# Keys of heads 0 to 3 of the second batch through the DMA crossbar, and a new order of crossings, joins, sends and loads around them

## The chip, the core and the metric

The kernel runs on one core of a Trainium2 chip. The metric is device time in microseconds (us) of one execution. "Span" is the profiled part of one execution, some 1.8 us shorter than its time; positions in a trace are counted from its start.

## The reference

Clustered attention (4 batches, 8 heads, 768 rows of 64), whose output goes straight into a mixture of 4 experts. A key counts for a query only where both have the same nearest centroid of 16.

```python
q_assign = argmax(einsum('bhsd,hcd->bhsc', q_n, c_n))      # keys likewise
mask = q_assign[:, :, :, None] == k_assign[:, :, None, :]
attn = softmax(where(mask, q @ k.T / sqrt(D), -1e9))
x = (attn @ v) as [3072, 512]
out = sum over e of p[:, e] * (relu(x @ w1[e]) @ w2[e])     # 4 experts, w1 512x1024, w2 1024x512
```

## The kernel before

Three jobs are interleaved. TensorE does the attention of a batch, the expert products of the batch before, and the preparation ("assignment") of the next batch: queries and keys must be turned so that head dimension lies along partitions, scored against the centroids, and their one-hot cluster numbers written below them as 16 more rows, so that one product gives both score and mask.

There are two ways to turn a float32 block. TensorE can do it against an identity (`turn`). Or it goes round TensorE: GpSimd splits the 32-bit values into two 16-bit halves (`split`), the DMA crossbar transposes the halves, issued by the SP queue (`cross`), and GpSimd joins them (`merge`):

```python
class Crossed(Assign):
    def split(self, n):
        if n == 0:
            self.h16 = self.halves(raws.tile([128, HG, QW], F32, name="h16", tag="raw"))
        ...                                            # cut: pool() copies, L361 or L364
    def cross(self, j):
        if j == 0:
            self.t16 = self.halves(raws.tile([128, HG, QW], F32, name="t16", tag="raw"))
        ...
        nc.sync.dma_start(out=self.t16[:, c]..., in_=self.h16[:, c]..., transpose=True)    # L371
    def merge(self, n):
        ...                                            # cut: pool() copies into self.all, L380
```

`h16` and `t16` come from the same ring of five buffers (`raws`) that queries, keys and values are loaded into. After the joins come the product with the centroids (`scores`, L267), its turn back (`back`, L276), the maximum and one-hot on VectorE (`top`), the crossing of the one-hot (`cross_onehot`, L426) and sixteen small DMAs that put it in place, issued by GpSimd (`send_all`, L336). GpSimd also issues the 1 MB loads of the expert weights (`load_w`, L153 and L154).

Preparation of a batch is a list of numbered items, taken one after the other between pieces of TensorE's main work. `put(n, f)` hangs `f` on item n; within an engine the order of items is the order of issue. For the second batch (b == 1), with y = 0 to 3 for keys of heads 0 to 3, queries of heads 0 to 3, keys of heads 4 to 7, queries of heads 4 to 7:

```python
g, z = divmod(y, 2)
if g == 0:
    for j in range(HG):
        put(4 * z + j, lambda x=x, j=j: turn(x, j))
else:
    for j in range(HG):
        put((8, 14)[z] + j, lambda x=x, j=j: x.split(j))
        put((13, 18)[z] + j, lambda x=x, j=j: x.cross(j))
        put((20, 24)[z] + j, lambda x=x, j=j: x.merge(j))
    ...
```

The softmax here doesn't subtract the row's maximum and nothing guards it: scores larger than these inputs give would overflow.

Of the kernel before, what the change touches and what calls it, by code (L numbers as in the profile page):

```python
# [20 lines left out]
def kernel(  # L21
# [27 lines left out]
    HG = H // 2  # L49
# [79 lines left out]
    def load_part(b, t, g, js=slice(0, HG), c=slice(0, A * D)):  # L129
        nc.sync.dma_start(  # L130
            out=raw[b, t, g][:, js, c],
            in_=(q, k, v)[t][b, g * HG:(g + 1) * HG]
            .rearrange("h (p a) d -> p h (a d)", p=128)[:, js, c])

    def take_raw():
        nonlocal loaded
        x = ORDER[loaded]
        loaded += 1
        raw[x] = raws.tile([128, HG, A * D], F32, name="raw")
        return x  # L140

    def load_raw(n=1, upto=len(ORDER)):
        for _ in range(n):
            if loaded < upto:
                load_part(*take_raw())

    def cast_v(b, g, js=range(HG)):
        for j in js:
            pool(VX[b % 2][:, g * HG + j, :, :D],
                 raw[b, 2, g][:, j, :].rearrange("p (a d) -> p a d", d=D))  # L150

    def load_w(e):
        nc.gpsimd.dma_start(out=W1[e], in_=moe_w1[e].rearrange("(i p) f -> p i f", p=128))  # L153
        nc.gpsimd.dma_start(out=W2[e], in_=moe_w2[e].rearrange("(i p) f -> p i f", p=128))  # L154
# [57 lines left out]
    class Assign:  # L212
# [23 lines left out]
        def turn(self, y, copy, shared=False):  # L236
            tp = self.bank()
            m, w = self.m, self.w
            for x in range(m):
                for i in range(self.i0, self.i1):  # L240
                    c0 = x * w + (i - self.i0) * 128
                    nc.tensor.matmul(tp[:, c0:c0 + 128],  # L242
                                     raw[self.b, self.t, self.g][:, y * m + x,
                                                                 i * 128:(i + 1) * 128],
                                     ident, is_transpose=True)
            if shared:
                t32 = moe.tile([128, DM], F32, name="t32q", tag="oacc", bufs=4)
            else:
                if self.all is None:
                    self.all = asg.tile([128, HG * QW], F32, name="t32", bufs=2)  # L250
                t32 = self.all[:, y * w:(y + 1) * w]
            copy(t32, tp[:, :m * w])
            self.t32s.append(t32)
# [63 lines left out]
        def put(self, j, r, on):  # L317

            p0 = 2 * CL * j
            self.move(self.rows(slice(D, D + CL), j, r),  # L320
                      self.ot[p0:p0 + CL, r * self.w:(r + 1) * self.w], on)
# [22 lines left out]
    class Crossed(Assign):  # L344
# [41 lines left out]
        def casts(self):  # L386
            y = self.g * HG // 2
            if self.b < ROWS:
                for r in range(2):
                    self.cast_half(r)  # L390
                return
            dve(late(self.t, self.b)[:, y:y + HG // 2], self.rows_of())
# [71 lines left out]
    def assigns(b):  # L464


        xs = [Crossed(b, t, g, (("misc",), ("mo",))[t == 0])
              for t, g in ((1, 0), (0, 0), (1, 1), (0, 1))]
        todo = {}

        def put(at, *fs):
            todo.setdefault(at, []).extend(fs)

        def turn(x, j):
            x.turn(j, dve)
            for r in range(2):
                x.cast(j, r, pool)

        if b == 1:
            for y, x in enumerate(xs):  # L480
                g, z = divmod(y, 2)
                if g == 0:
                    for j in range(HG):
                        put(4 * z + j, lambda x=x, j=j: turn(x, j))
                else:
                    for j in range(HG):
                        put((8, 14)[z] + j, lambda x=x, j=j: x.split(j))
                        put((13, 18)[z] + j, lambda x=x, j=j: x.cross(j))
                        put((20, 24)[z] + j, lambda x=x, j=j: x.merge(j))
                    put((24, 28)[z], x.take_all)  # L490
                    for r in range(2):
                        put(28 + 3 * z + r, lambda x=x, r=r: x.cast_half(r))
                at = (8, 29)[g]
                put(at, lambda x=x: x.scores(dve))
                put(at + 1 + z, x.back, x.top, x.scale_onehot, x.cross_onehot)
                put(at + (4, 5)[g] + z, x.send_all)
            put(1, lambda: load_w(2))
            put(3, lambda: load_raw(upto=11))
            put(20, lambda: cast_v(b, 0))
            put(22, lambda: load_raw(2, upto=13))  # L500
            put(24, lambda: load_w(3))
            put(30, lambda: cast_v(b, 1))

        for y, x in enumerate(xs if b > 1 else ()):
            z = y % 2
            t = 8 * y
            for j in range(HG):
                put(t + j, lambda x=x, j=j: x.split(j))
                put(t + 2 + j, lambda x=x, j=j: x.cross(j))
                put(t + 9 + j, lambda x=x, j=j: x.merge(j))  # L510
            put(t + 6, load_raw)
            put(t + 15 + 4 * z, x.casts)
            at = 16 * (y // 2) + 24
            put(at, lambda x=x, t=("mo", "misc")[z]: x.scores_split(t))
            put(at + 2 + 6 * z, x.cross_scores)
            put(at + 5 + 6 * z, x.merge_scores)
            if b < ROWS:
                put(at + 9 + 6 * z, x.top, x.scale_onehot, x.cross_onehot)
                put(at + 13 + 6 * z, x.send_all)
                continue  # L520
            put(at + 9 + 6 * z, x.top, x.number, x.cross_numbers)
            put(at + 12 + 6 * z, x.store_numbers)
            put(at + 14 + 6 * z, x.spread_numbers)
        for g in range(2 if b > 1 else 0):
            for j in range(HG):
                put(36 + 8 * g + j, lambda g=g, j=j: cast_v(b, g, (j,)))
            put(40 + 8 * g, load_raw)
        for at in range(XSTEPS[b]):
            for f in todo.pop(at, []):
                f()  # L530
            yield
        assert not todo
# [248 lines left out]
    NSTEP = B * UB * PER_U + PAUSE  # L781
    PER_B = UB * PER_U
    LEAD = 6
    XSTEPS = [0, 38, 63, 63]
    step = 0
    gens = []

# [101 lines left out]
    def late_queries():  # L889
        load_raw()  # L890
        for y in (0, 1):
            qd.turn(y, dve, True)
            yield
        casts(qd, (0, 1))
        load_raw(3)
        qd.scores(dve)
        yield
        qd.back()
        qd.top()
        yield  # L900
        qd.onehot()
        qd.keep()
        qd.send_all()
        yield
    S1 = PER_U + PAUSE
    gens.append(Paced(late_queries(), 5, S1 - 6, S1 + 4))
    for b in range(1, B):
        gens.append(Paced(assigns(b), XSTEPS[b], PER_B * (b - 1) if b > 1 else S1 + 7,
                          PER_B * b - 2 if b > 1 else S1 + 55))
# [54 lines left out]
```

## Time and profile before

| | before |
|---|---|
| time, median of 3 | 472.60 us |
| TensorE busy | 463.2 of 470.4 us |
| TensorE's share of the chain that ended last | 95% |
| GpSimd busy | 194.8 us |
| VectorE busy | 227.4 us |

The number to read is the first of TensorE: the kernel is a row of matmuls with hardly a gap. Two rows of the page, in 40 equal slices of the span (11.8 us each; a digit is tenths), show the same for the whole length: busy share, then granted clock.

```profile
PE   8999999999999999999999999999999999999996
PEclk9999999999999999999999999999999999999999
```

The list of TensorE's waits (engine, tile, line, releaser: total us, times, longest) has only small entries. This, its largest, is from the first microseconds.

```profile
PE ps_s L87 <- DVE blank L80: 1.2, 1, 1.2
```

Two stretches of the SP queue (start, duration, line, operation): the second batch's second keys are loaded, and their crossings come right behind the one-hot crossings.

```profile
33.97 0.46 SPq L130 DMA_DIRECT2D raw<-in_k_dram  x1
...
57.03 2.79 SPq L426 DMA_TRANSPOSE oht<-oh  x2
59.93 2.57 SPq L371 DMA_TRANSPOSE t<-h  x2
```

### The profile page before, as it was taken

How to read it: one execution, taken by the hardware profiler on the slowest of the kernel's cores; microseconds unless marked ns; L12 is line 12 of the kernel's file. 1: busy time of each engine (PE TensorE's matmuls, PEld its weight loads, DVE VectorE, ACT ScalarE, POOL GpSimd, SP SyncE). 2: the span in 40 equal slices, each digit the busy share in tenths (PEclk: the TensorE clock that was granted, in tenths of full speed). 3: DMA queues.
4: the chain of work that ended last, by engine and by line, in shares of the span. 5: the costliest groups of instructions: out<-in, count | busy, mean ns of one | idle time of the engine just before them, and what ended most of it. 6: DMA issues, size and time to landing. Idle time of an engine off the chain costs nothing.

```text
span 470.4 us, 11349 instructions
## 1 busy us (share of the span) xinstructions
PE 463.2 (98%) x4505; PEld 329.1 (70%) x4505; DVE 227.4 (48%) x554; ACT 276.9 (59%) x502; POOL 194.8 (41%) x301
## 2 busy tenths in 40 slices
PE   8999999999999999999999999999999999999996
PEld 5778777767767766777776667766766666667665
DVE  5964723542325563321234463523778767674112
ACT  5767675445655655566565656656665675664342
POOL 5936779275355593450433942000233232230000
PEclk9999999999999999999999999999999999999999
DMA  8999966996645941503666844220100100100101
GB/s 277 262 211 339 216 99 120 236 127 182 144 68 127 182 114 32 144 18 61 169 123 127 133 106 151 71 75 11 52 13 8 54 11 10 33 29 11 46 2 45
DMA packets 82381, 49.85 MB, mean 106 GB/s; under 512 B 57944, under 2 KB 77080, under 8 KB 82328
## 3 DMA queue, kind: packets, MB, share of 16 engines
q1 hardware_dynamic: 73080, 39.80, 35.1%
q0 software_dynamic: 8576, 9.25, 11.0%
q8 instruction: 35, 0.57, 0.5%
q14 instruction: 18, 0.15, 0.1%
q10 hardware_dynamic: 672, 0.08, 0.1%
HBM read 37.31 MB, written 6.30 MB: 93 GB/s over the span
## 4 chain that ended last, share of the span: by engine, by line
PE 95%; DVE 2%; DMA 1%; issue 0%; ACT 0%; SPq 0%; ACTq 0%
PE ps_mo L739 36%; PE ps_mo L758 35%; PE ps_s L649 9%; PE ps_av L676 7%; PE ps_s L562 1%; DMA kf<-oht 1%; PE ps_misc L562 1%; PE ps_s L87 1%; PE ps_mo L406 1%; PE ps_mo L242 1%; PE ps_misc L406 1%; DVE kf L315 1%; PE ps_misc L242 1%; PE ps_mo L267 0%; PE ps_misc L267 0%; DVE oh L287 0%
## 5 line engine op out<-in xcount | busy, mean ns | idle before, releaser
L655 ACT ACTIVATE at<-ps_s 128x512 bf16<-128x512 f32 x252 | 147.6, 596 | 115.5 <-PE ps_s L649 100.1
L739 PE MATMUL ps_mo<-xT,w1b 128*128 128x256 bf16 (+1 forms) x1664 | 195.9, 264 | 0.0
L758 PE MATMUL ps_mo<-w2b,hT 128*128 128x512 bf16 (+2 forms) x784 | 190.0, 375 | 0.0
L739 PEld LDWEIGHTS <-w1b 128*128 128x128 bf16 x1664 | 146.1, 98 | 24.8 <-issue 1.2
L745 ACT ACTIVATE hT<-ps_mo 128x512 bf16<-128x512 f32 x192 | 114.7, 598 | 60.5 <-PE ps_mo L739 57.7
L767 DVE SCALAR_TENSOR_TENSOR oacc<-ps_mo,psb,oacc 128x512 f32<-128x512 f32 (+1 forms) x74 | 54.3, 734 | 125.3 <-PE ps_mo L758 125.1
L758 PEld LDWEIGHTS <-hT 128*128 128x128 bf16 x784 | 66.9, 98 | 57.8 <-issue 3.1
L649 PE MATMUL ps_s<-qf,kf 80*128 80x256 bf16 (+1 forms) x456 | 82.7, 267 | 0.8 <-ACT at L655 0.4
L676 PEld LDWEIGHTS <-at 128*128 128x128 bf16 x1152 | 69.9, 97 | 15.3 <-issue 1.7
L676 PE MATMUL ps_av<-vx,at 128*128 128x65 bf16 x1152 | 80.3, 193 | 0.0
L662 POOL TENSOR_TENSOR at<-at,same 128x512 bf16<-128x512 bf16 x24 | 28.2, 1177 | 98.5 <-ACT at L655 83.0
L649 PEld LDWEIGHTS <-kf 80*128 80x128 bf16 x456 | 42.1, 98 | 20.6 <-issue 1.4
L380 POOL COPY t<-t 128x768 uint16<-128x768 uint16 x40 | 44.3, 1127 | 0.0
L579 DVE TENSOR_SCALAR same<-qf,late 128x256 bf16<-128x256 bf16 x144 | 39.0, 323 | 0.0
L662 DVE TENSOR_TENSOR at<-at,same 128x512 bf16<-128x512 bf16 x48 | 21.6, 450 | 25.9 <-ACT at L655 25.9
L364 POOL COPY h<-raw 128x768 uint16<-128x768 uint16 x24 | 20.3, 864 | 30.4 <-DMA raw<-in_k_dram 16.7
L361 POOL COPY h<-raw 128x768 uint16<-128x768 uint16 x16 | 13.1, 829 | 39.3 <-DMA raw<-in_q_dram 32.3
L765 DVE TENSOR_SCALAR oacc<-ps_mo,psb 128x512 f32<-128x512 f32 x18 | 13.5, 748 | 27.0 <-PE ps_mo L758 27.0
L683 DVE RECIPROCAL zr<-ps_av 128x4 f32<-128x4 f32 (+1 forms) x50 | 8.9, 178 | 33.3 <-PE ps_av L676 33.2
L336 POOL DMA_DIRECT2D qf<-oht x40 | 20.4, 519 | 7.5 <-DVE oht L313 3.9
L422 POOL COPY st<-sct 128x384 uint16<-128x384 uint16 x16 | 11.0, 736 | 28.8 <-DMA sct<-scs 28.8
L685 DVE TENSOR_TENSOR xn<-ps_av,zr 128x256 bf16<-128x256 f32 (+1 forms) x50 | 20.7, 414 | 1.7
(130 smaller groups left out, 263.2 us busy)
## 6 DMA issues: line engine op xcount, KB each, us to landing
raw<-in_v_dram SPq DMA_DIRECT2D x8, 768.0 KB, 5.4
out_dram<-oacc SPq DMA_DIRECT2D x23, 256.0 KB, 2.0
raw<-in_k_dram SPq DMA_DIRECT2D x7, 768.0 KB, 7.5
raw<-in_q_dram SPq DMA_DIRECT2D x6, 768.0 KB, 5.7
w1b<-in_moe_w_dram POOLq DMA_DIRECT2D x4, 1024.0 KB, 12.3
w2b<-in_moe_w_dram POOLq DMA_DIRECT2D x4, 1024.0 KB, 17.6
qf<-nos SPq DMA_DIRECT2D x2, 768.0 KB, 5.2
xT<-xn SPq DMA_TRANSPOSE x80, 2.4
```

The source lines that it names most:

```text
L336: (nc.gpsimd if self.b or self.i0 and self.g else nc.sync).dma_start(out=self.rows(slice(D, D + CL), j, r), in_=self.oht[p0:p0 + CL, :self.w])
L380: pool(self.all[:, y * w:(y + 1) * w].bitcast(U16)[:, z::2], self.t16[:, (2 * z + y) * w:(2 * z + y + 1) * w])
L579: nc.vector.tensor_scalar(same[:, x * 256:(x + 1) * 256], clusters(b)[:, g, w, k // 2, k % 2, :], key_nos[b % 2][:, g, 8 * i + 4 * (k // 2 ...
L649: nc.tensor.matmul(sp[:, x * n:(x + 1) * n], KF[b % 2][:K, h, r, i * 128:(i + 1) * 128], QF[b % 2][:K, h, rs[0]:rs[-1] + 1, w * 128:(w + 1 ...
L655: nc.scalar.activation(at, sp, ACT.Exp, scale=scale)
L662: (nc.gpsimd if n4 in POOL_STEPS else nc.vector).tensor_tensor(at, at, same_cluster(b, w, cur), op=ALU.mult)
L676: nc.tensor.matmul(av[:, h % 2, m, :], at[:, c0:c0 + 128], VX[b % 2][:, h, 2 * i + r, :], start=(first and x == 0 and m == 0), stop=(last ...
L685: nc.vector.tensor_tensor(xn[:, :nr].rearrange("p i j d -> p j i d"), av[:, :, :, :D], zr.broadcast_to([128, 2, nr, D]), op=ALU.mult)
L739: nc.tensor.matmul(ph[:, x * n:(x + 1) * n], W1[e][:, i, (f + x) * 128:(f + x + 1) * 128], xT[:, i, :], start=(i == 0), stop=(i == ND - 1))
L745: nc.scalar.activation(ht, ph, ACT.Relu)
L758: nc.tensor.matmul(po, hT[f // per][:, c0:c0 + 128], W2[e][:, f, c], start=(f == 0), stop=(f == NF - 1))
L767: nc.vector.scalar_tensor_tensor(oacc[:, c], po, pap, oacc[:, c], op0=ALU.mult, op1=ALU.add)
```

## The change

The intent is to take twelve float32 turns from TensorE, the engine that bounds the kernel, and to give the keys of heads 0 to 3 the way round it that those of heads 4 to 7 already take. All the rest of the diff re-times what hangs on it: the crossings of heads 4 to 7 stand right behind the one-hot crossings of heads 0 to 3, the key joins ahead of the sends, and the loads of the third and fourth experts later.

```diff
-                if g == 0:
-                    for j in range(HG):
-                        put(4 * z + j, lambda x=x, j=j: turn(x, j))
-                else:
-                    ... (8, 14) split, (13, 18) cross, (20, 24) merge, take_all, cast_half
-                at = (8, 29)[g]
+                for j in range(HG):
+                    if y == 1:
+                        put(2 + j, lambda x=x, j=j: turn(x, j))
+                        continue
+                    put((0, 0, 15, 19)[y] + j, lambda x=x, j=j: x.split(j))
+                    put((1, 0, 17, 21)[y] + j, lambda x=x, j=j: x.cross(j))
+                    put((11, 0, 24, 33)[y] + j, lambda x=x, j=j: x.merge(j))
+                ... take_all at (14, 0, 27, 36), cast_half at (17, 0, 37, 41)
+                at = (14, 39)[g]
                 put(at, lambda x=x: x.scores(dve))
                 put(at + 1 + z, x.back, x.top, x.scale_onehot, x.cross_onehot)
-                put(at + (4, 5)[g] + z, x.send_all)
-            put(1, lambda: load_w(2))
-            put(3, lambda: load_raw(upto=11))
-            put(20, lambda: cast_v(b, 0))
-            put(22, lambda: load_raw(2, upto=13))
-            put(24, lambda: load_w(3))
-            put(30, lambda: cast_v(b, 1))
+                put((28, 44)[g] + z, x.send_all)
+            put(6, lambda: load_raw(3, upto=11))
+            put(8, lambda: load_w(2))
+            put(32, lambda: cast_v(b, 0))
+            put(31, lambda: load_w(3))
+            put(34, lambda: load_raw(2, upto=13))
+            put(42, lambda: cast_v(b, 1))
...
-    XSTEPS = [0, 38, 63, 63]
+    XSTEPS = [0, 48, 63, 63]
...
-        load_raw(3)
+        load_raw()
```

Cuts are marked with dots. `XSTEPS` is the number of items; they are spread over the same 48 steps of TensorE's main work, so an item number doesn't stand for the same moment before and after. The last line makes room in the ring of five: `h16` and `t16` of heads 0 to 3 need two of its buffers, so three loads wait until item 6.

## The prediction

> **What bounds the kernel now.** I read the page first: busy shares, then the chain that ended last, then the waits of TensorE alone.
>
> ```profile
> PE 463.2 (98%) x4505; PEld 329.1 (70%) x4505; DVE 227.4 (48%) x554; ACT 276.9 (59%) x502; POOL 194.8 (41%) x301
> ...
> PE 95%; DVE 2%; DMA 1%; issue 0%; ACT 0%; SPq 0%; ACTq 0%
> ```
>
> The first line is busy time by engine, the second the chain by engine. TensorE carries 95% of the chain; of 470.4 us it is idle for 7. Busy alone would prove little, so I looked whether its matmuls stand at an even pace: twenty 256-wide ones of the first expert product (L739) take 2.18 us in the chain (0.109 each) wherever they stand, and sixteen 512-wide ones (L758) 3.45 us (0.216 each). No stretch shows them spread out, so the end is set by the sum of TensorE's work. Outside the first microseconds its longest listed wait is 0.4 us (the second batch's first keys and queries are never waited for). So time falls only where TensorE gets less to do, and rises where something it needs comes late.
>
> **What the turns cost.** The change takes TensorE's float32 turns away from the keys of heads 0 to 3 of batch 1. The timeline of TensorE shows the first of those four turns between its neighbours (start, duration, line, operation):
>
> ```profile
> 41.10 0.28 PE L676 MATMUL ps_av<-vx,at 128*128 128x65 bf16 x4
> 41.22 0.52 PE L242 MATMUL ps_misc<-ident,raw 128*128 128x128 f32 x3
> 41.58 0.59 PE L758 MATMUL ps_mo<-w2b,hT 128*128 128x512 bf16 x2
> ```
>
> Durations overlap in the pipeline; starts tell the price. From 41.22 to 41.58 the three transposes of one head hold TensorE 0.36 us, 0.12 each. The other three turns start at 43.26, 44.41 and 45.92 and their successors at 43.59, 44.79 and 46.28: 0.33, 0.38 and 0.36.
>
> **The Trainium skill.** (1) "Perfetto Trace Analysis", Identifying the Most-Contended Engine, says matmul busy time is a poor measure of distance to the limit; agreed, hence the start-to-start readings above. (2) "TensorE: Matmul & The Clock Gate", Part 4: PE-mode transpose, has some 275 ns for one transpose in a kernel's context. The trace has 273 ns as a listed duration but 0.12 us from start to start; the latter is what is saved. (3) "DMA: Bandwidth & Descriptors", DMA Transpose (X-bar), allows 2-byte types only, which is why float32 keys are split into 16-bit halves on GpSimd (L364), crossed, and joined again (L380); the trace shows these three steps for heads 4 to 7. (4) The same page, Issuing engines are not separate DMA queues, says that all DMAs share the same 16 engines; the trace agrees: transposes that land in 2.8 us as a rule took 13.4 us when issued among the weight and value loads at 80 us.
>
> **The change part by part.**
> Removed: 4 turns of 3 transposes, 0.36+0.33+0.38+0.36 = 1.43 us of TensorE. Also 4 VectorE copies out of PSUM (0.555 each, 2.2 us) and 8 GpSimd casts (0.50, 4 us); both engines have room (48% and 41%), so these count nothing themselves.
> Added: 4 splits (0.83, 3.3 us) and 4 joins (1.13, 4.5 us) on GpSimd, 4 crossings on the SP queue (1.25 us of issue, 2.8 to land), 2 half casts on VectorE (about 1 to 1.3 each). Net GpSimd +3.8 us, VectorE about even. None is on TensorE.
> Moved: the score and back-turn matmuls of both head groups go later, at the same number. Score matmuls of heads 0 to 3 stood at 52.2 us, and after stand behind the first query-side turn of the next stage, near 56.8 us. The sends of heads 0 to 3 go behind the splits of all of heads 4 to 7 and the joins of their keys; the last expert's weight load goes behind those sends; the values of heads 0 to 3 and the joins of the queries come after it.
> On the path: -1.43 us, so 472.6 - 1.4 = 471.2 us if no new wait appears.
>
> **Does a new wait appear?** I laid the new order of GpSimd and SP out with durations from this trace (an estimate).
> Heads 0 to 3: splits from 42.0 us, the last at about 46.7 as the query casts stand between; last crossing landed by 49.6; joins 51.5 to 55.5, behind the load of the third expert. TensorE asks at 56.8. About 1 us to spare.
> Heads 4 to 7: their keys land near 55, splits of keys and queries end near 62. SP is in order: it first waits for the two one-hot crossings of heads 0 to 3 (until about 64.4), then issues two key crossings, two output crossings, the other two: 72. Joins end near 75.4, sixteen sends of 0.48 us near 83, so the last weights are issued at 83 and 84. Before, they went out here:
>
> ```profile
> 74.81 3.90 POOL L380 COPY t<-t 128x768 uint16<-128x768 uint16 x4
> 78.64 0.80 POOL L153 DMA_DIRECT2D w1b<-in_moe_w_dram  x1
> 79.44 0.91 POOL L154 DMA_DIRECT2D w2b<-in_moe_w_dram  x1
> 80.33 3.73 POOL L380 COPY t<-t 128x768 uint16<-128x768 uint16 x3
> ```
>
> The issues of that stretch (size, microseconds to landing), and TensorE's first use of these two weights (98.16 and 100.31):
>
> ```profile
> w1b<-in_moe_w_dram POOLq DMA_DIRECT2D x1, 1024.0 KB, 12.8
> w2b<-in_moe_w_dram POOLq DMA_DIRECT2D x1, 1024.0 KB, 18.5
> ```
>
> ```profile
> 98.16 0.61 PE L739 MATMUL ps_mo<-xT,w1b 128*128 128x128 bf16 x8
> ...
> 100.31 1.04 PE L758 MATMUL ps_mo<-w2b,hT 128*128 128x512 bf16 x4
> ```
>
> The second weight lands at 79.4 + 18.5 = 97.9, 2.4 us before its use. After the change it is issued some 4.5 us later and asked for 1.4 us sooner, at 98.9. With the same 18.5 us it lands at 102.4: 3.5 us of stall. With 13.5, the fastest landing of the four such loads, it lands at 97.5: none. The value and key loads that shared the engines with it before now start some 3 us behind it (they wait for a buffer that the value cast frees at about 86.7), so I put the landing at 99 to 102. The first weight (needed near 96.4, due at 92 to 96) should just make it. The score matmuls of the second group (asked for near 90, query joins ending near 90.6) have no slack either, but a delay there moves the weight's demand by as much, so the two don't add up.
>
> **The rivals.**
> A, clean saving: all of it hides, 471.2 us. For it: every part stands off TensorE, and the positions look set by hand to just fit. Against: a margin of 2.4 us before becomes about nothing.
> B, a late last weight: TensorE stalls 1 to 3.5 us near 99 us and the saving is given back: 472.2 to 474.7. For it: the ordering above. Against: the landing may be quicker, and my GpSimd times may be 2 us late.
> C, late joins: TensorE waits at the score matmuls of heads 0 to 3 (57 us) or 4 to 7 (90 us), 0 to 2 us: 471 to 473. For it: joins cost 0.93 to 1.24 us and my slack is about 1 us or less.
> D, keys of heads 4 to 7 late: the next batch's key load (issued near 87, 13.0 us to land before) holds GpSimd until 100, so sends end near 113 and land near 116; needed at 122. Unlikely to bite; if it did, several microseconds.
> E, VectorE: it now has two half casts between one-hot and normalisation; at 65 us before it idled 4.4 us, so nothing.
>
> **Range and chances.** A alone gives 471.2; B and C together have perhaps an even chance, with a mean of some 1.5 us when they happen. I take 471.9 us: the full saving less about half of it. Runs of the kernel before spread by 0.45 us. Low end 470.8 (clean, a little more off the path than I counted), high end 474.2 (a stall of 3 us). A 2% change is 9.5 us: the saving can't be that large since only 1.43 us of work goes; a loss that large needs two of the rivals at their worst. Chances: faster 0.01, same 0.97, slower 0.02.
>
> **What would show it.** TensorE should have 12 float32 transposes less and 1.4 us less from start to start between 40 and 56 us. If A is right, its waits list nothing above 0.5 us past the first stage, and the weight product at the fourth expert's start (L758) begins near 98.9. If B, there is a gap or stretched run just ahead of it, ended by the landing of the second weight, and the load's issue stands near 84. If C, the wait stands at L267 and is ended by GpSimd's L380. The prediction is wrong if the batch's change shows a wait of more than 4 us, or if the crossings land so late among the loads that the sends slip past 113 us.

## The result, and the profile after

The changed kernel took 476.45 us (median of 4 runs, 475.93 to 476.54), the kernel before 472.42 us in the same rounds: 4 us more. Ratios here are close to the mean time of one kernel's fast runs over that of the other's in the same rounds, so not quite the ratio of the medians; this one is 1.0083, with a 95% interval of 1.0065 to 1.0100. That is within 2%, as the prediction held most likely, but outside its range and on the other side of the kernel before.

The page after, for the rows shown above: busy time, the two strips, and the chain.

```profile
PE 464.8 (98%) x4493; PEld 328.9 (69%) x4493; DVE 224.8 (47%) x552; ACT 277.0 (58%) x502; POOL 197.4 (42%) x301
...
PE   7999999799999999999999999999999999999997
PEclk9999999989999999999999999999999999999999
...
PE 90%; POOL 4%; DVE 2%; DMA 2%; issue 1%; ACT 1%; SPq 0%; ACTq 0%; POOLq 0%
```

The twelve turns are gone (4505 to 4493 matmuls), yet the eighth slice (83 to 95 us) has a 7, the clock has an 8 in the ninth, and GpSimd has come into the chain with 4%. One place, then, not a general slowdown. To see it exactly I matched the score matmuls of the attention of both traces one by one and took the difference of their starts. It begins at +0.4 us in this run and stands at +0.5 before the first removed turn (kernels with the same beginning show -0.2 to +0.5 at the start). At the four places of the removed turns it falls by 0.33 to 0.36 each, to -0.94 where the kernel before is at 51.7 us; 0.3 are given back by 63 us (-0.66), so some 1.2 us are gained. At 95.7 it is +3.87, from 101 on +4.58 to the end. The work removed does save time. All the loss arises between 90 and 101 us.

The waits of TensorE and of its weight loads in the changed kernel name the cause:

```profile
PE ps_mo L267 <- POOL t L380: 2.5, 2, 1.4
...
PEld ps_mo L267 <- POOL t L380: 3.9, 2, 2.1
```

The two rows are of the same standstill, seen at the matmuls and at the loads ahead of them, so they don't add up. TensorE's timeline shows it; the bracket at the end is the idle time just before and its releaser:

```profile
90.74 0.85 PE L267 MATMUL ps_misc<-t,bdc 128*32 128x384 f32 x8
93.04 0.84 PE L267 MATMUL ps_mo<-t,bdc 128*32 128x384 f32 x4 [1.45 <-POOL t L380]
94.95 1.15 PE L267 MATMUL ps_mo<-t,bdc 128*32 128x384 f32 x4 [1.07 <-POOL t L380]
96.03 1.89 PE L739 MATMUL ps_mo<-xT,w1b 128*128 128x256 bf16 x8
97.71 1.98 PE L758 MATMUL ps_mo<-w2b,hT 128*128 128x512 bf16 x6
99.53 0.38 PE L649 MATMUL ps_s<-qf,kf 80*128 80x256 bf16 x2
```

The score products of the keys of heads 4 to 7 (`ps_misc`) run; those of the queries (`ps_mo`) wait for joins. Where nothing waits, the same sixteen products hold TensorE 1.43 us (in this trace from 57.41 to 58.84, for heads 0 to 3). Here L739 would have started at 90.74 + 1.43 = 92.17; it started at 96.03. That is 3.86 us. The list shows only 2.5 us of it as idle: the eight query products, released by the joins in two lots, took two more rounds of some 0.34 us than in the undisturbed place, and the last two ran at half clock already (0.79 us each, not 0.49). The next fourteen matmuls then took 99.53 - 96.03 = 3.50 us; at the usual pace they take 8 x 0.109 + 6 x 0.216 = 2.17. The view by stretches says why (stretch, its length, busy time of TensorE, its weight loads, VectorE, ScalarE and GpSimd, granted clock, DMA share, GB/s):

```profile
95.34:98.76 3.42, 3.42 (x15) 1.64 (x12) 0.56 (x1) 0.60 (x1) 3.42 (x6) 0.50 1.20 203
```

For 3.4 us behind the standstill the clock was granted at half (0.50); in the stretch behind, to 104 us, it is 1.00 again. The sum: +0.5 at the start, -1.2 gained, +3.86 at the standstill, +1.33 of half clock behind it, about +4.5, as the matched matmuls say. (The Trainium skill, "TensorE: Matmul & The Clock Gate", Part 1, states that the gate falls to half after at least one idle window of about 3.4 us. The length of the half-clock stretch agrees; the condition only in part: see the end.)

Why the joins came so late is told by GpSimd's timeline of the changed kernel, and by the SP queue's:

```profile
77.57 1.05 POOL L380 COPY t<-t 128x768 uint16<-128x768 uint16 x1 [0.73 <-DMA t<-h]
78.53 3.87 POOL L336 DMA_DIRECT2D kf<-oht  x8
82.40 4.43 POOL L336 DMA_DIRECT2D qf<-oht  x8
86.82 0.83 POOL L153 DMA_DIRECT2D w1b<-in_moe_w_dram  x1
87.62 0.93 POOL L154 DMA_DIRECT2D w2b<-in_moe_w_dram  x1
88.52 2.53 POOL L149 CAST vx<-raw 128x384 bf16<-128x384 f32 x4
91.00 3.90 POOL L380 COPY t<-t 128x768 uint16<-128x768 uint16 x4
```

```profile
48.90 0.54 SPq L130 DMA_DIRECT2D raw<-in_k_dram  x1
...
61.80 3.80 SPq L426 DMA_TRANSPOSE oht<-oh  x2
65.76 3.59 SPq L371 DMA_TRANSPOSE t<-h  x2
...
72.00 8.70 SPq L371 DMA_TRANSPOSE t<-h  x6
```

GpSimd works in order and without a gap from 77.57 on: last key join, sends, weight issues, values, query joins. It ends at 94.9, where TensorE had begun the score products at 90.7. All of it starts only when the key crossings are through, and these start late: the second keys' load is issued at 48.90 (before: 33.97), their own splits end at 59.2 (those of the queries at 62.5), and SP, in order, issues the one-hots first, at 61.8. Two pairs of crossings took 3.8 and 3.6 us where the pairs before took 2.8 and 2.6.

### The profile page after: what moved, and what is told of

Same layout as the page of the kernel before. It is cut to its first block, busy times and chain, and to the rows that moved or that the text cites. A ratio compares the mean times of both kernels' runs of the same rounds, so it can differ in the third digit from the quotient of the medians.

```text
span 474.8 us, 11327 instructions
## 1 busy us (share of the span) xinstructions
PE 464.8 (98%) x4493; PEld 328.9 (69%) x4493; DVE 224.8 (47%) x552; ACT 277.0 (58%) x502; POOL 197.4 (42%) x301
## 4 chain that ended last, share of the span: by engine, by line
PE 90%; POOL 4%; DVE 2%; DMA 2%; issue 1%; ACT 1%; SPq 0%; ACTq 0%; POOLq 0%
PE ps_mo L758 34%; PE ps_mo L739 33%; PE ps_s L649 9%; PE ps_av L676 7%; POOL t L380 2%; PE ps_s L562 1%; DMA kf<-oht 1%; POOL qf L336 1%; PE ps_misc L562 1%; POOL kf L336 1%; PE ps_s L87 1%; PE ps_mo L242 1%; PE ps_mo L406 1%; DMA t<-h 1%; PE ps_mo L267 1%
## 5 line engine op out<-in xcount | busy, mean ns | idle before, releaser
L739 PE MATMUL ps_mo<-xT,w1b 128*128 128x256 bf16 (+1 forms) x1664 | 196.6, 265 | 0.0
L739 PEld LDWEIGHTS <-w1b 128*128 128x128 bf16 x1664 | 146.4, 98 | 25.1 <-issue 1.1
L380 POOL COPY t<-t 128x768 uint16<-128x768 uint16 x44 | 46.9, 1087 | 12.1 <-PE ps_s L649 8.7
L364 POOL COPY h<-raw 128x768 uint16<-128x768 uint16 x28 | 22.6, 830 | 23.2 <-DMA raw<-in_q_dram 14.8
L361 POOL COPY h<-raw 128x768 uint16<-128x768 uint16 x16 | 13.1, 832 | 37.5 <-DMA raw<-in_q_dram 30.9
```

What stands on the lines that cost most here:

```text
L364: pool(self.h16[:, z * HG * QW + c:z * HG * QW + c + 2 * QW], self.halves(raw[self.b, self.t, self.g])[:, 2 * c:2 * c + 4 * QW][:, z::2])
L380: pool(self.all[:, y * w:(y + 1) * w].bitcast(U16)[:, z::2], self.t16[:, (2 * z + y) * w:(2 * z + y + 1) * w])
L739: nc.tensor.matmul(ph[:, x * n:(x + 1) * n], W1[e][:, i, (f + x) * 128:(f + x + 1) * 128], xT[:, i, :], start=(i == 0), stop=(i == ND - 1))
```

## The experiments

Two causes were in view from the start. **J**, late joins, is what the trace shows. **W**, a late last weight, was the prediction's fear; the trace shows no wait for it, but that says little: the second weight landed at 87.62 + 16.0 = 103.6 us, and TensorE, which asked at 104.89, would without the 3.86 + 1.33 us have asked near 99.7. The rivals to both: that the path through the crossbar itself is at fault, and that all that is lost is a matter of order.

The shift of matched matmuls against the kernel before, in us, for the kernels that are read by it (start: where the kernel before is at 40 us):

| kernel | start | 62 to 79 us | about 99 to 101 us | end |
|---|---|---|---|---|
| changed kernel | +0.5 | -0.7 | +4.2 to +4.6 | +4.6 |
| score products two later | 0.0 | -1.2 | -1.2 to +2.7 | +3.6 |
| keys on TensorE again | 0.0 | +0.1 | +2.5 to +3.1 | +3.1 |
| next keys' load early | -0.1 | -1.4 | -1.7 to +1.3 | +1.3 |
| weights among the sends | +0.5 | -0.8 | -1.1 to -0.7 | +2.1 |
| third batch's keys first | +0.3 | -1.0 | -1.2 to -0.9 | -0.8 |

### 1. One-hot crossings behind the key crossings

```diff
-put((1, 0, 17, 21)[y] + j, lambda x=x, j=j: x.cross(j))
+put((1, 0, 15, 21)[y] + j, lambda x=x, j=j: x.cross(j))
-put(at + 1 + z, x.back, x.top, x.scale_onehot, x.cross_onehot)
+put(at + 1 + z, x.back, x.top, x.scale_onehot)
+put((19, at + 1)[g] + z, x.cross_onehot)
```

> Edit: the one-hot crossings of heads 0 to 3 are issued behind the key crossings of heads 4 to 7 instead of ahead of them; nothing else. Theory J (late joins: TensorE stood still near 91 to 95 us at the query score matmuls of heads 4 to 7, because GpSimd's query joins ended at 94.9; they were late because the key joins, which stand ahead of sixteen sends and two weight issues, waited for crossings that the SP queue held back behind the one-hot crossings): key joins end near 66 to 70 instead of 78.5, query joins near 84 to 88, no wait at L267 over 0.3 us, no half-clock stretch, time 470.9 to 472.0. Theory X (the extra crossings and splits of heads 0 to 3 are themselves too much for GpSimd or the DMA engines): GpSimd's work is the same, so the joins stay late and the time stays at 475 or more.

Measured: 477.61 us (477.46 to 479.09), ratio 1.0118. The expectation missed. Issued earlier, the crossings fell among loads in flight; the SP queue, and TensorE's longest wait:

```profile
56.45 14.86 SPq L371 DMA_TRANSPOSE t<-h  x4
```

```profile
PE ps_mo L759 <- DMA w2b<-in_moe_w_dram: 3.3, 1, 3.3
```

Four issues took 14.9 us, where they took 5.4 in the changed kernel's quiet stretch at 43 us. The key joins ended at 75.7, near where I had predicted them for the change itself; the wait for the query joins shrank from 2.5 to 2.1 us, and W appeared behind it with 3.3. So both causes exist, and swapping two crossings mends neither.

### 2. Score products of heads 4 to 7 two items later

```diff
-at = (14, 39)[g]
+at = (14, 41)[g]
```

> Edit: the score matmuls of heads 4 to 7 two schedule steps later, GpSimd's order unchanged. Theory J: TensorE asks near 96 us instead of 91, the joins end near 95, so that wait and the half clock vanish (471 to 472 if nothing stands behind it). Theory W (the last expert's weights, issued at 86.8 and 87.6, are late too and were only hidden by the joins' wait): with the joins' wait gone TensorE stops near 99 to 100 us for weights landing near 103 to 105, so 473 to 476 remains, with a gap ahead of the fourth expert's second product.

Measured: 475.78 us (475.08 to 476.72), ratio 1.0075.

```profile
PE ps_mo L739 <- DMA w1b<-in_moe_w_dram: 2.0, 1, 2.0
```

L267 no longer waits for L380. The fourth expert's first weight now comes 2.0 us too late, the second one 0.6, and there is a half-clock stretch again (from 97.4 us). TensorE kept its 1.2 us up to 98.6 us and then lost 4.8. W stands right behind J: taking one away uncovers the other.

### 3. Keys of heads 0 to 3 on TensorE again, all else as in the change

```diff
-if y == 1:
-    put(2 + j, lambda x=x, j=j: turn(x, j))
+if y < 2:
+    put((0, 4)[y] + j, lambda x=x, j=j: turn(x, j))
...
-if y != 1:
+if y > 1:
```

> Edit: the keys of heads 0 to 3 are turned on TensorE again as before; all the re-timing of heads 4 to 7, of loads, sends and weights stays as in the change. If the re-timing is at fault (J), the joins of heads 4 to 7 end about as late (91 to 95 us), TensorE asks about 1 us later, so a wait of 2 to 4 us stays: 475 to 478. If the crossbar path of heads 0 to 3 is at fault (X), time falls back to the kernel before, 472 to 473.

Measured: 475.23 us (474.38 to 476.31), ratio 1.0061.

```profile
PE ps_mo L267 <- POOL t L380: 1.8, 1, 1.8
```

The last key join ended at 78.4 us, as in the changed kernel, and the query joins near 94.8. So the loss needs nothing of the crossing of heads 0 to 3; the re-timing alone makes it. Where the kernel before is at 51.7 us, this one has a shift of 0.0 and run 2 one of -1.44: that difference is the twelve turns. At 63 us they stand at +0.1 and -1.2, so about 0.1 of what is given back there is the re-timing's, too. One thing more can be read here: without `h16` and `t16` of heads 0 to 3 the second keys were loaded at 33.96 us, as early as in the kernel before, and yet their crossings went out only at 66.1, behind the one-hots (62.6). An early load alone doesn't mend the joins while the one-hots stand first; by run 1, moving the one-hots alone doesn't either.

### 4. Last expert's weights ahead of the sends

```diff
-put(31, lambda: load_w(3))
+put(27, lambda: load_w(3))
```

> Edit: the last expert's two weight loads are issued ahead of the sixteen sends of heads 0 to 3 (near 79 us instead of 87) instead of behind them; joins keep the same work ahead of them on GpSimd. Theory J: the wait at the query score matmuls stays, 476 to 477. Theory W alone: the stall goes, 471 to 473.

Measured: 488.52 us (487.35 to 488.96), ratio 1.0338. A miss by 11 us, on GpSimd's timeline:

```profile
79.80 2.95 POOL L336 DMA_DIRECT2D kf<-oht  x6
87.80 1.02 POOL L336 DMA_DIRECT2D kf<-oht  x1 [5.05 <-DMA w1b<-in_moe_w_dram]
96.73 0.48 POOL L336 DMA_DIRECT2D kf<-oht  x1 [7.91 <-DMA w2b<-in_moe_w_dram]
```

DMAs of one queue take their completion semaphores in turn from a set of eight in this kernel: the records show numbers 117 and 118 for the two weights, 111 to 116 for six sends, then 117 again, which waits for the load that has it. The seventh and eighth send thus waited for two 1 MB loads, and the query joins behind them came at 103 us. TensorE stood 14 us, and the clock was at half from about 93 to 110 us. This doesn't refute W; the edit brought in a wait of its own.

### 5. Third expert's weights seven items earlier

```diff
-put(8, lambda: load_w(2))
+put(1, lambda: load_w(2))
```

> Edit: the third expert's weight loads go out behind the second split of heads 0 to 3 (near 44 us) instead of near 50. Theory D (the key crossings of heads 4 to 7 are slow because four loads, 4.3 MB, issued within 48 to 52 us keep the DMA engines full until about 70 us): the loads end some 5 us sooner, key joins end at 72 to 76 instead of 77 to 78.5, the wait for the query joins shrinks to 0 to 2 us. But the crossings of heads 0 to 3 now run among the weight loads, so a new wait at their score matmuls (57 us) of 0 to 4 us may appear. Time 472 to 476. If the one-hot crossings ahead in the SP queue are the cause instead, the key joins stay at 77 to 78.

Measured: 482.03 us (480.75 to 482.79), ratio 1.0195 (at 2% unclear, as run 8). Missed: instead of freeing the way for the second crossings, the weights were in the way of the first.

```profile
43.28 13.03 SPq L371 DMA_TRANSPOSE t<-h  x4
```

Four crossings, 13.0 us instead of 5.4; score products of heads 0 to 3 waited 5.7 us in all, and the key joins ended at 85.2.

### 6 to 8. Values later

The edits of three runs in one:

```diff
-put(6, lambda: load_raw(3, upto=11))
+put(6, lambda: load_raw(2, upto=10))
+put(25, lambda: load_raw(upto=11))          # 6, 7, 8: values of heads 0 to 3 behind the crossings
-put(32, lambda: cast_v(b, 0))
+put(37, lambda: cast_v(b, 0))               # 7, 8: their cast behind the query joins
-put(8, lambda: load_w(2))
+put(1, lambda: load_w(2))                   # 8 only
-at = (14, 39)[g]
+at = (17, 39)[g]                            # 8 only
```

> Edit: the values of heads 0 to 3 are loaded behind all crossings of heads 4 to 7 (near 80 us) instead of with their keys and queries (50 us). Theory D: 0.77 MB less in flight, so the key crossings land 2 to 4 us sooner, key joins end near 74 to 76, query joins near 91 to 92, a wait of at most 1.5 us, time 472 to 474.5 with the last weights issued near 83 to 84. If loads in flight don't matter: joins and time as in the change, 476.

> Edit: as the run before, and the value casts of heads 0 to 3 stand behind the query joins on GpSimd instead of ahead. Theory J: query joins end another 1.9 to 2.5 us sooner, near 89 to 90, before TensorE asks at about 91, so nothing is left at the query score matmuls. What then remains is theory W: last weights issued near 83 to 84, first needed near 96.6 and 99, stall 0 to 3 us. Time 471.2 to 474.

> Edit: as the run before, the third expert's weights at 44 us as in the first run of this call, and the score matmuls of heads 0 to 3 three schedule steps later so that their joins may be late. If D, J and W are the whole story every wait goes: last weights issued near 80, no wait above 0.6 us past the first stage, full clock, time 471.0 to 471.9, faster than both kernels.

| run | us (low to high) | ratio | TensorE's longest wait past 2 us from the start |
|---|---|---|---|
| 6 | 476.49 (474.71 to 479.91) | 1.0096 | 1.8 at L276, 1.6 at L267 |
| 7 | 477.07 (476.95 to 480.42) | 1.0123 | 3.8 at the last weight |
| 8 | 481.99 (480.03 to 487.12) | 1.0220 | 3.7 at L267, heads 0 to 3 |

The value load out of the way brought the key joins from 78.6 to 76.9 us and J down to 1.6. With the cast behind the joins, J was gone (query joins end at 91.2), and W took its place in full:

```profile
PE ps_mo L759 <- DMA w2b<-in_moe_w_dram: 3.8, 1, 3.8
```

This is the prediction's rival B, a little above its size, in a kernel where nothing else hides it. Run 8 repeats the error of run 5. The spread of these three is wide (7 us in run 8), so I read their traces, not their last microsecond. The clock takes part in that spread: executions of one and the same kernel differ in the granted clock, in run 6 from 0.993 (479.91 us) to 1.000 (475.74 us).

### 9. The second keys' load early

Here `t16` of heads 0 to 3 is claimed already at the split, which shifts the ring by one place, so that the second keys can be loaded at 33.9 us as in the kernel before; the value load and its cast are later as in run 7, the one-hot crossings behind the key crossings as in run 1. The diff shows only what is new.

```diff
+if (self.b, self.t, self.g) == (1, 1, 0):
+    self.t16 = self.halves(raws.tile([128, HG, QW], F32, name="t16", tag="raw"))
...
-put(6, lambda: load_raw(3, upto=11))
+put(0, lambda: load_raw(upto=9))
+put(6, lambda: load_raw(upto=10))
+put(25, lambda: load_raw(upto=11))
```

> Edits: the ring slots for the crossed keys of heads 0 to 3 are claimed before the keys of heads 4 to 7 are loaded, so that this load goes out at 34 us again, ahead of the first crossings; the values of heads 0 to 3 load behind all crossings (80 us) and are cast behind the query joins; one-hot crossings of heads 0 to 3 behind the key crossings of heads 4 to 7. Theory: the key joins were late for two causes in parallel, the one-hot crossings ahead in the SP queue and the loads that fill the DMA engines; mending one alone gained nothing. With both gone only the third expert's 2 MB (issued at 50) is in flight under the key crossings: key joins end at 64 to 70, sends end by 78, last weights issued near 76 to 79, query joins by 86; no wait over 0.5 us past the first stage, full clock, 470.9 to 472.0. If the two causes are not the whole of it, key joins stay at 75 or later and time at 474 or more.

Measured: 473.24 us (472.60 to 473.48), ratio 1.0015 [1.0000, 1.0030]: 3 us of the 4 are back. Key joins end at 71.5, query joins at 86.9, and one wait is left:

```profile
PE ps_mo L763 <- DMA w2b<-in_moe_w_dram: 2.5, 1, 2.5
```

The clock was full throughout. TensorE runs 1.4 to 1.7 us ahead of the kernel before up to 98.6 us and loses 3 us at the last weight, issued at 82.0 and landing 19.5 later. With the key load early, the values out of the way and the one-hots behind the keys J is gone without moving anything on TensorE; what remains is W alone. Which of the edits this needs is not separated: run 7, with the values alone, was rid of J too, but with joins 4 to 5 us later.

### 10 and 11. The third expert's weights later, on top of run 9

```diff
-put(8, lambda: load_w(2))
+put(18, lambda: load_w(2))      # 10;  11: put(23, ...)
```

> Edit: as the run before, and the third expert's weights are issued behind the key splits (near 57 us) instead of near 50, so that most of the key crossings run on idle DMA engines. Key joins end at 62 to 66. The weights land at 70 to 76, needed at 78.7 and 82, but the eight-deep rotation of GpSimd's DMA semaphores may make the last sends wait for them. 470.9 to 472.0; if the crossings are still caught by the weights, 473 to 476.

> Edit: as the run before, the third expert's weights behind the query splits too (near 60 us). Key crossings wholly free of loads, key joins end at 61 to 64; the seventh and eighth send then wait for the weights' landing (72 to 78 us), last weights issued near 80 to 82, landing near 98 to 99, when TensorE asks: stall 0 to 2 us. 471 to 474.

Run 10: 473.43 us (473.18 to 473.78), ratio 1.0021. The third weights met the key crossings (joins end at 75.6), and several waits below 1 us ate what W gave back. Run 11: 476.30 us (476.01 to 477.70), ratio 1.0079. Without loads around them four key crossings took 5.2 us and the joins ended at 66.4, but a wait appeared that nobody had expected. The wait of TensorE, VectorE's timeline, and GpSimd's:

```profile
PE ps_mo L744 <- DVE oacc L772: 3.6, 1, 3.6
```

```profile
61.53 3.99 DVE L436 TENSOR_SCALAR oh<-oh 128x384 bf16<-128x384 bf16 x1
```

```profile
62.45 3.97 POOL L382 COPY t<-t 128x768 uint16<-128x768 uint16 x4
```

One small VectorE operation that takes 0.26 us as a rule lasted 3.99, from GpSimd's issue of the second weight (61.56 us) until the third of its four back-to-back joins was done (65.4). The Trainium skill, "SBUF — State Buffer", Who interferes with whom, says that a VectorE `tensor_scalar` in a two-port mode and a GpSimd instruction take a shared pair of ports by turns, and the second one fully blocks. The records fit that; I made no run to test it, so it is an explanation, not a finding.

### 12. The last weights among the sends

On top of run 9, the weights go out behind ten of the sixteen sends, so that the six left behind them don't reach the loads' semaphores (run 4). The one-hot crossings of heads 0 to 3 also stand one item earlier (18, not 19), which the diff leaves out.

```diff
-put((28, 44)[g] + z, x.send_all)
+if y == 1:
+    put(29, lambda x=x: x.send_all((0,)), lambda: load_w(3),
+        lambda x=x: x.send_all((1, 2, 3)))
+else:
+    put((28, 44)[g] + z, x.send_all)
```

> The version with the next batch's keys loaded early (473.24), with the one-hot crossings of heads 0 to 3 one item earlier and the last expert's weights issued after ten of the sixteen sends instead of after all. Theory (W, the last weight, is all that this version still lost at 98 us): weights issued some 3 us earlier, near 77 to 79, the wait for the second weight falls from 2.5 to 0.5 us or less, the six sends left behind the loads are not asked for before 120 us, and the time is 471.0 to 472.3. Rival (the weights land by what else is on the engines, not by when they are issued): they land as late as before, wait 2 to 3 us, 473 to 474. Rival (the sends left behind wait for a semaphore of a load, as they did with the loads ahead of all sends): GpSimd stands more than 4 us at a send and the query joins end after 95: 475 or more.

Measured: 473.58 us (473.23 to 474.99, 6 runs), ratio 1.0030. The weights were issued at 76.9 and 77.8, and the wait for them is gone, as expected; the time is not what was expected. A third wait has taken over, first in TensorE's list, with GpSimd's timeline:

```profile
PE ps_misc L408 <- POOL t L382: 1.5, 1, 1.5
```

```profile
101.77 1.55 POOL L366 COPY h<-raw 128x768 uint16<-128x768 uint16 x1 [5.38 <-DMA raw<-in_k_dram]
```

The third batch's keys landed at 101.7 us (before: 79.25 + 13.0 = 92.3), so its whole preparation ran 5 us or more late until L408, near 141 us, asked for it.

### 13 and 14. Order of the loads behind

The prediction having missed, two more runs were spent on the one question left: is this third wait again a matter of order, or is there no room on the DMA engines between 76 and 102 us? Both build on run 12.

```diff
+ORDER[11:13] = ORDER[12], ORDER[11]        # 13: third batch's keys ahead of values of heads 4 to 7
-put(42, lambda: cast_v(b, 1))
+put(46, lambda: cast_v(b, 1))              # 13: and the cast of those values later
-put(25, lambda: load_raw(upto=11))
+put(20, lambda: load_raw(upto=11))         # 14: values of heads 0 to 3 earlier
```

> The version with the weights among the sends (473.58), with the third batch's keys loaded ahead of the values of heads 4 to 7 and these values cast behind the splits of those keys. Theory (order of the loads is all that is left): the key load lands near 95 us, its splits follow at once, the wait of 1.5 us at the score products near 141 us is gone, the shift against the kernel before stays at -0.7 us or better to the end: 471.0 to 472.2. Rival (no room on the DMA engines): it lands at 98 or later, or the values of heads 4 to 7 now come late near 122 us; the time stays at 473 to 475.

> The version with the weights among the sends (473.58), with the values of heads 0 to 3 loaded five items earlier, between the crossings of the keys and of the queries of heads 4 to 7. Theory (order of the loads is all that is left): the value load leaves the crowd at 79 us, values of heads 4 to 7 and the third batch's keys land some 3 us sooner, near 98 us, and the time is 471.5 to 473.0. Rival (no room on the DMA engines): the query crossings slow down by as much, the key joins or the sends shift by 2 us or more, and the time stays at 473 to 475.

Run 13: 471.87 us (470.88 to 474.49, 6 runs), where the kernel before took 472.52 in the same rounds; ratio 0.9996, interval 0.9976 to 1.0017. Its profiled run (471.11 us) has a span of 469.3 us, 1.1 below that of the kernel before. GpSimd's timeline:

```profile
98.93 3.16 POOL L367 COPY h<-raw 128x768 uint16<-128x768 uint16 x4 [6.02 <-DMA raw<-in_k_dram]
```

The keys were split some 3 us sooner than in run 12 (not at 95, as I had put it, but soon enough), no wait above 0.6 us is left past the first microseconds, and the shift goes from +0.3 to -0.8 and stays there: a saving of about 1.1 us, kept to the end. But one of six runs took 474.49, so the version is not shown to beat the kernel before; its margins are thin, and which one broke in the slower runs I can't say, for only one run has a trace (the granted clock was 1.000 in all six, so it was not the clock).

Run 14: 473.73 us (472.77 to 479.49), ratio 1.0059. The rival's outcome: the values slowed the query crossings, GpSimd stood 5.6 us before the last query join, and L267 waited 1.5 us again. Two of its six executions took 479.0 and 479.5 us, at a granted clock of 0.993 and 0.992, where the other four show 0.999 or 1.000: the half clock set in in some executions of one kernel and not in others.

## Why the prediction was wrong

**The saving** was right: 1.43 us from four start-to-start readings, 1.44 measured between runs 2 and 3. What the sum left out is that 0.1 to 0.3 us of it is given back before 63 us. (A slip without effect: the first weight's demand, put near 96.4, is 98.16 - 1.43 = 96.7 by the prediction's own figures.)

**"Does a new wait appear?"** is the step that failed, in its sizes. The order on each engine was as laid out, and so was the first half: joins of heads 0 to 3 ran from 52.2 to 56.2 (predicted 51.5 to 55.5), TensorE asked at 57.4 and did not wait. Then:

| | predicted, us | after, us |
|---|---|---|
| splits of heads 4 to 7 end | 62 | 62.5 |
| one-hot crossings issued | 64.4 | 65.6 |
| key joins end | 75.4 | 78.6 |
| sends end | 83 | 86.8 |
| query joins end | 90.6 | 94.9 |
| TensorE asks | 90 | 90.7 |

The largest term is crossings among loads: I gave each issue 1.25 us, from a quiet stretch, though the same text quotes that crossings among loads take longer to land. The two one-hots ended 1.2 us after the 64.4 laid out (3.80 us of issue; 2.79 before), the first two key crossings took 3.6, not 2.5 (one alone 2.33), and the last key crossing took 4.2 us from issue to its join, which is some 0.6 more than laid out (75.4 less one join, less an issue at 70.75). The second two took 2.5, as predicted. That is about 2.9 of the 3.2 us at the joins. The sends (8.3 us for 16, not 7.7) and the value cast (2.5, not 1.9) add 0.6 each. Each addition is small, but the prediction itself had found "no slack" at this place, so every microsecond of error was to be paid in full; it allowed 0 to 2 us and the standstill was 3.9. So what failed is the estimate of the SP queue and of GpSimd behind it; that the score products wait for L380 was named as rival C.

**The clock** was left out. The half-clock stretch adds 1.3 us to this stall, and no line of the profile before could show it, as that kernel never stands still.

**Rival C** was therefore the one that came, at twice its size. **Rival B** was real but hidden behind it, as the prediction's sentence about the two not adding up says; runs 2, 7 and 9 uncovered it with 2.6, 3.8 and 2.5 us, in or next to the 1 to 3.5 foreseen, at another order of loads in runs 7 and 9. One detail of B was wrong: the next value and key loads did not start 3 us behind the weights but 3 us ahead of them (83.4 and 83.9 us). **Rival A** is what the traced execution of run 13 shows: with all three late things mended the saving does stay. **D** did not bite; the late key load that it feared did, but in run 12 alone and at another place, the third batch's own products with the centroids. **E** did not show in the changed kernel: VectorE is never in its list of TensorE's waits with more than 0.6 us past the first stage.

**The range** was too narrow by the prediction's own working: B's upper end, 474.7, lay above its high end of 474.2, and a margin of "about nothing" at two places, each behind a dozen estimated durations, called for more room upward.

## What to carry to other kernels

Where a profile shows no wait, it shows no slack either: before taking work from the bounding engine, list for every producer how long before its use it is done, and take the durations from a stretch as crowded as the one it will move into. Crossings go out more slowly among large loads (four of them: 5.4 us in a quiet stretch, up to 14.9 among loads), and what stands on one issuing queue goes out in order, so an item moved by a few places can slow all behind it; a wait removed at one place should be expected to come out at the next-latest one. A stall of two to four microseconds on TensorE can cost more than its length, since the clock may be granted at half behind it, and whether it is can change from one execution to the next.

## What the Trainium skill lacked or had wrong

- "TensorE: Matmul & The Clock Gate", Part 1, has in its table of states the clock fall to half after an idle window of about 3.4 us. The half-clock stretches here were 3.41 us long, or twice that (runs 5, 8, 11), or five times (17.07, run 4). But the window need not be idle. I cut each trace, from its first full clock on, into intervals of 3.413 us; every half-clock stretch begins at such a border. In the 24 full-clock intervals just before one (8 inside a program, 16 at the programs' ends) TensorE was listed busy for at most 42%; in the other 2161 full-clock intervals of all sixteen traces, none of which a half-clock stretch followed, for at least 49%. The lines (TensorE's busy time is the number behind the length) are of the changed kernel, of run 2, and of run 9, whose wait of 2.5 us was divided between this interval and the next (52% and 73%) and did not set it off:

```profile
91.93:95.34 3.41, 1.23 (x8) 0.29 (x8) 0.29 (x1) 0.00 (x0) 3.41 (x5) 1.00 1.12 212
```

```profile
93.95:97.36 3.41, 1.42 (x13) 0.69 (x12) 0.80 (x2) 0.00 (x0) 3.41 (x6) 1.00 1.15 209
```

```profile
97.36:100.77 3.41, 1.78 (x30) 1.60 (x27) 2.46 (x6) 1.79 (x3) 3.37 (x4) 1.00 1.22 192
```

So in these traces it mattered where a wait fell, not only how long it was. This was read out of the traces afterwards; no run was made to test it, and nothing here tells what happens between 42 and 49%.

- "TensorE: Matmul & The Clock Gate", Part 4, gives a transpose some 275 ns in context. As a duration that agrees (273 ns is listed for the float32 ones here), but it is not their price: among other matmuls they cost 0.12 us each from start to start, and twelve of them removed saved 1.44 us, the same 0.12 each.
- "DMA: Bandwidth & Descriptors" has no figure for how a crossing fares among loads. Four issues took 5.2 to 5.5 us in a quiet stretch (the changed kernel, runs 1, 2 and 11) and 10.9 to 14.9 us among weight and other loads (runs 1, 5, 9), and it is the issuing queue that is held, so that everything behind it on SP is late too.
- No page was found to mention that small DMAs issued behind large ones can wait for a semaphore they are to reuse: eight in turn on GpSimd's queue here, 5.05 and 7.91 us of standing (run 4).
- "SBUF — State Buffer" has the shared ports of VectorE and GpSimd block for one instruction. In run 11 a VectorE operation of 0.26 us lasted 3.99, past three GpSimd copies in a row; whether that is the same block is not settled here.
